# Sending decays and rows from GpSimd, and naming two experts earlier, in a recurrence followed by a routed expert layer

## The chip, the cores and the metric

The kernel runs on one core of a Trainium2 chip. The metric is the device time of one execution in microseconds; the median of three runs of the kernel before is 436.33 us (435.48 to 436.64). The profile is of one more execution.

## The reference

A gated recurrence over 768 steps makes tokens, and each token then goes through one of 16 experts:

```python
q, k, v, f_logit: (4, 8, 768, 48) float32
f = 1 / (1 + exp(-f_logit))
for t in range(768):                       # per batch and head, state is 48 x 48
    state = f[t][:, None] * state + outer(k[t], v[t])
    y[t] = q[t] @ state
x = y.transpose(0, 2, 1, 3).reshape(3072, 384)

g_idx = argmax(x @ w_group)                # 4 groups, softmax weight g_w
e_idx = argmax(x @ w_expert[g_idx])        # 4 experts of the group, softmax weight e_w
out[token] = g_w * e_w * (relu(x @ w1[g, e]) @ w2[g, e])     # w1 384 x 1024, w2 1024 x 384
```

All is float32 in and out. One expert has two weight tensors of 1.5 MB each.

## The kernel before

**The recurrence, in 12 units.** The 768 steps are cut into 6 chunks of 128. A unit is one chunk of two of the four batches: units 2c and 2c+1 make up chunk c. A unit's work is cut into stages, each a generator that emits some instructions at every call: `l` loads f, k, q and v (SyncE's queue, four transfers of 384 KB in rows of 192 bytes), `c` bounds f on VectorE, `g` makes the decays (`gated`: exponential and logarithm on ScalarE, the cumulative sum `cs` as a matmul at L574, two exponentials into `eq` and `kh`, L575 and L576, and a DMA of the last decay row, 4 KB, into `ends`, L581), `m` multiplies q and k by the decays on VectorE (`multiplied`), `t` transposes them on TensorE and copies them out on ScalarE (`turned`, L604 and L605), `s` makes the scores `ap` (L630) and masks them into `am` on VectorE (L633), `n` updates the state, `w` makes the output (`weighed`: matmuls from the state at L669, then from `am` at L674, copied to `xT` at L677), `d` makes the router's logits (`done`: L689, copied to `lgT` at L691, folded at L694), and `x` transposes the output back into token rows (`listed`: L709, copied at L710) and sends 384 KB of them to `x_dram` with a DMA (L712). Stage `b` (`decayed`) transposes the four rows of `ends` of a chunk on TensorE (L614), once in every odd unit.

**The order.** TensorE, VectorE and ScalarE run in the order in which the program emits the stages; the lists `BEGIN`, `EVEN`, `ODD` and `ORDERS` write it down by hand. `"g+1"` is one call of stage g for the next unit. SyncE and GpSimd are ordered by a scheduler from the same program. The queues are strictly in order: a DMA that an engine issues waits in that engine's queue with everything behind it. ScalarE issues the `ends` and `x_dram` transfers, SyncE the loads, the weights and the 4 KB `meta` writes, GpSimd the indirect gathers and scatters.

**Routing.** When both units of a chunk have logits, `routed(c)` starts, a generator that is called by the letter `r`. Its calls are: 1 and 2 the best group and expert as a one-hot `ohe` (L189 to L200); 3 the rank of each token within its expert by matmuls (`rk`, L205 and L208); 4 adds the count so far (L214 to L217); 5 and 6 the operands of a table of token numbers; 7 the routing weight, written with the token's number as `meta` into the last two columns of `x_dram` (L245 to L247: VectorE, a GpSimd copy, a SyncE DMA); 8 the table's matmul (`tb`, L252); then the table is added up.

**The early experts.** After the fourth chunk (`CLOSE` = 3) the two fullest experts are ranked (`ranked`, L272 to L281), named in `who` (L287 to L290), and 128 of their tokens each are taken as `rows_e` (L313 to L319). SyncE reads `who`, and loads each one's `w1` and `w2` (`load_weights`); GpSimd gathers the 128 rows of each from `x_dram` with their `meta` (L394). Calls named `e` then emit: the transposes of the first gather (`turn_in`, L430), of the second, the first layer of both experts (`up`, L440) and the second layer of both (`down_rows`, L457). These stand in the last list, `ORDERS[NU]`, between the routing calls of the last two chunks.

**The experts.** When all is routed, 16 further passes go through the experts, widths 230 down to 174 tokens, each with the two layers (L440 and L472), gathers, transposes in and out on VectorE, and scatters (L451). The weights have two buffers and one more, and are loaded some passes ahead.

Of the kernel before, what the change touches and what calls it, by code (L numbers as in the profile page):

```python
# [23 lines left out]
def kernel(  # L24
# [155 lines left out]
    def route(c, lg, sb, tabled=True, tidy=None, ranking=None):  # L180
# [36 lines left out]
        nc.vector.tensor_tensor(run, run, rk[:, B, :], OP.add)  # L217
        yield
# [94 lines left out]
    def choose_early(sb):  # L313
        number = numbers(sb)
        mine = sb.tile([P, EARLY, GE], FP32, tag="mine2", bufs=1, name="mine2")
        nc.vector.tensor_tensor(mine, order[:, 0:EARLY, :], number[:, :, 0].unsqueeze(1).broadcast_to((P, EARLY, GE)), OP.mult)
        got = sb.tile([P, EARLY], FP32, tag="got2", bufs=1, name="got2")
        nc.vector.reduce_sum(out=got, in_=mine, axis=AX)
        nc.vector.tensor_copy(rows_e, got)  # L319
        named(EARLY, sb)  # L320
# [59 lines left out]

    def load_weights(pool, ap):
        e = value(ap, GE - 1)
        w1 = pool.tile([P, KO, F], FP32, tag="w1", name="w1")
        nc.sync.dma_start(out=w1, in_=w1v[bass.ds(e, 1)].rearrange("o p k f -> (o p) k f"))
        w2 = pool.tile([P, FO, DM], FP32, tag="w2", name="w2")
        nc.sync.dma_start(out=w2, in_=w2v[bass.ds(e, 1)].rearrange("o p k f -> (o p) k f"))
        return w1, w2
# [113 lines left out]
    with ExitStack() as fast:  # L501
# [33 lines left out]

        SRC = {"f": f_logit, "k": k, "qh": q, "v": v}
# [21 lines left out]
        def gated(i):  # L558
# [13 lines left out]
            for b in range(2):  # L572
# [4 lines left out]
                if b:  # L577
# [3 lines left out]
                    nc.scalar.dma_start(out=ends[c][2 * s:2 * s + 2, :], in_=eq[P - 1:P].rearrange("o b h d -> o b (h d)"))  # L581
                yield

        def multiplied(i):

            w = live[i]
            for b in (slice(0, 1), slice(1, 2)) if i < 2 else (slice(0, 2),):
                qh, kh = heads(w["qh"][:, b])[:, :, 0:D], heads(w["kh"][:, b])[:, :, 0:D]
                nc.vector.tensor_tensor(qh, qh, heads(w["eq"][:, b])[:, :, 0:D], OP.mult)
                yield  # L590

                nc.vector.scalar_tensor_tensor(out=kh, in0=kh, scalar=math.exp(SAFE), in1=heads(w["k"][:, b]), op0=OP.min, op1=OP.mult)
                yield

        def turned(i):
# [4 lines left out]
            for b in range(2):  # L600
                for nm in ("q", "k"):
                    pt = bank([P, HP, P], "tr_" + nm)
                    for a in range(HP):
                        nc.tensor.transpose(out=pt[:, a, :], in_=w[nm + "h"][:, b, 2 * a:2 * a + 2, :].rearrange("t r d -> t (r d)"), identity=ident)  # L604
                    (nc.vector.tensor_copy if i == 0 and b == 0 and nm == "k" else nc.scalar.copy)(w["T" + nm][:, b], pt)  # L605
                    yield
# [94 lines left out]
        def listed(i):  # L701
# [10 lines left out]
            nc.scalar.dma_start(out=rows_of(c, 2 * s, 2)[:, :, 0:DM], in_=x.rearrange("t b a r d -> t b (a r d)"))  # L712
            yield

        def routed(c):

            yield from route(c, groups[c], sb, tidy=fix_early if c == CLOSE + 1 else None, ranking=rank_early if c == CLOSE else (lambda pool: ranked(GE, pool)) if c == NC - 1 else None)
            if c == CLOSE:
                choose_early(sb)
                for p in range(EARLY):  # L720
                    weights[p] = load_weights(wp, who[0:1, p:p + 1])
# [5 lines left out]
        def advance(gens):  # L727
# [11 lines left out]
            d0 x1 x1 t2 t2 t2 t2 c3 g3 g3 x1 s2 s2 s2 s2 g3 g3 w2 d1 w2 n2 m3 m3 c4 g4 g4""".split()  # L739
# [4 lines left out]
            NU - 2: "d-2 r r r x-1 x-1 t t t t g+1 g+1 x-1 r s s s s w d-1 w n m+1 m+1 r r".split(),  # L744
            NU - 1: "d-2 b n-1 x-1 x-1 r r t t t t x-1 r s s s s r w d-1 w r r".split(),
# [261 lines left out]
```

## Time and profile before

| | us |
|---|---|
| median of three runs | 436.33 (435.48 to 436.64) |
| the profiled execution's own time | 435.97 |
| its span, first to last instruction | 434.2 |
| TensorE, matmuls busy | 409.4 (94%) |
| TensorE, weight loads busy | 383.8 (88%) |
| VectorE busy | 268.5 (62%) |
| ScalarE busy | 154.5 (36%) |
| GpSimd busy | 71.7 (17%) |
| granted TensorE clock, mean | 0.986 |

The first 145 us are the recurrence and its routing, and the rest is the experts; the early experts lie from 141.9 to about 169.5 us. A line of the timeline holds: start, duration (both us from the span's start), engine, program line, operation, names, shapes, count, and in brackets how long the engine stood idle before it and what released it. PE is TensorE's matmuls, PEld its weight loads, DVE VectorE, ACT ScalarE, POOL GpSimd and SP SyncE; ACTq, POOLq and SPq are these engines' queues, that is instructions that count as no work, such as the issue of a DMA. Matmuls are pipelined and their ends are modelled, so a busy PE says little, while a gap before a PE or PEld line is time in which TensorE had to wait. Line numbers are those of the kernel before.

### The profile page before, as it was taken

The numbers are of one execution on the slowest core, as the hardware profiler recorded it, in microseconds if no ns is written. First come the engines' busy times: TensorE is split into PE (matmuls) and PEld (weight loads), VectorE is DVE, ScalarE is ACT, GpSimd is POOL, SyncE is SP. The second block draws the span as 40 slices with busy tenths as digits, with TensorE's granted clock in tenths as the row PEclk, the third lists the DMA queues.
The fourth block names the chain that finished last, engine by engine and source line by source line (L and its number), as shares of the span: only waits on it lengthen the run. The fifth ranks groups of instructions, "written<-read, shape, count | busy, mean of one in ns | idle before, by whom it ended". The sixth has DMA issues, their size and how long they took to land. (4 is left out here: it accounts for less than half of the span.)

```text
span 434.2 us, 10159 instructions
## 1 busy us (share of the span) xinstructions
PE 409.4 (94%) x4103; PEld 383.8 (88%) x4103; DVE 268.5 (62%) x781; ACT 154.5 (36%) x338; POOL 71.7 (17%) x109
## 2 busy tenths in 40 slices
PE   4999999999998989999999999999999999999960
PEld 2888999889998877989999999999999999999940
DVE  5675786778687841540799759468559558651500
ACT  5676765576664411211123123123123122222200
POOL 3000000000002037101031232212212211022120
PEclk9999999999999999999999999999999999999995
DMA  9999999999815979965728549468459558652010
GB/s 168 175 208 203 186 196 161 219 217 209 159 39 166 404 242 364 394 217 215 255 74 337 170 189 327 151 238 311 158 233 348 174 191 331 239 163 92 25 32 17
DMA packets 135232, 88.97 MB, mean 205 GB/s; under 512 B 105422, under 2 KB 125972, under 8 KB 135178
## 3 DMA queue, kind: packets, MB, share of 16 engines
q1 hardware_dynamic: 126754, 72.38, 61.2%
q0 software_dynamic: 5056, 11.06, 7.6%
q10 hardware_dynamic: 3368, 4.80, 3.1%
q8 instruction: 34, 0.56, 0.6%
q14 instruction: 20, 0.16, 0.1%
HBM read 78.71 MB, written 9.83 MB: 204 GB/s over the span
## 5 line engine op out<-in xcount | busy, mean ns | idle before, releaser
L440 PE MATMUL hp<-xe,w 128*128 128x128 f32 (+14 forms) x864 | 138.6, 320 | 1.6 <-DMA w<-in_moe_w_dram 1.6
L440 PEld LDWEIGHTS hp<-xe,w 128*128 128x128 f32 x864 | 135.8, 190 | 2.5 <-issue 1.7
L472 PE MATMUL yo<-h,w 128*128 128x230 f32 (+13 forms) x672 | 115.8, 333 | 0.0
L472 PEld LDWEIGHTS yo<-h,w 128*128 128x128 f32 x672 | 113.7, 190 | 0.2
L423 DVE STREAM_TRANSPOSE yr<-yT 32x192 f32<-32x192 f32 (+1 forms) x208 | 70.5, 339 | 64.7 <-ACT yT L473 62.1
L441 ACT ACTIVATE h<-hp 128x256 f32<-128x256 f32 (+14 forms) x72 | 34.4, 478 | 110.7 <-PE hp L440 110.7
L416 DVE STREAM_TRANSPOSE xe<-xg 32x192 f32<-32x192 f32 (+1 forms) x208 | 69.7, 335 | 5.0 <-PE hp L440 2.0
L451 POOL DMA_INDIRECT out_dram<-yt,xg x32 | 34.5, 1080 | 154.7 <-ACT yt L448 82.2
L473 ACT COPY yT<-yo 128x230 f32<-128x230 f32 (+13 forms) x42 | 13.5, 326 | 80.5 <-PE yo L472 80.5
L394 POOL DMA_INDIRECT xg<-x_dram,rows_p x30 | 29.6, 988 | 70.4 <-DMA out_dram<-yt,xg 22.8
L633 DVE TENSOR_TENSOR am<-ap,tri 128x512 f32<-128x512 f32 x48 | 29.8, 683 | 18.0 <-PE ap L630 18.0
L574 PE MATMUL cs<-ld_f,tri 128*128 128x384 f32 x48 | 19.2, 526 | 6.2 <-DVE ld_f L555 5.4
L630 PE MATMUL ap<-Tq,Tk 48*64 48x128 f32 x768 | 23.9, 273 | 0.1
L674 PE MATMUL y<-am,v 128*64 128x128 f32 x384 | 23.1, 273 | 0.0
L674 PEld LDWEIGHTS y<-am,v 128*64 128x64 f32 x384 | 21.3, 137 | 0.5 <-DVE am L633 0.5
L630 PEld LDWEIGHTS ap<-Tq,Tk 48*64 48x64 f32 x768 | 20.8, 133 | 1.0 <-issue 0.2
L457 PE MATMUL yo<-w,h 128*128 128x384 f32 x64 | 21.3, 486 | 0.0
L246 POOL COPY meta<-token 128x4 int32<-128x4 int32 x6 | 1.3, 218 | 109.0 <-DMA x_dram<-meta 109.0
L457 PEld LDWEIGHTS yo<-w,h 128*128 128x128 f32 x64 | 11.9, 190 | 7.4
L574 PEld LDWEIGHTS cs<-ld_f,tri 128*128 128x128 f32 x48 | 8.6, 200 | 10.4 <-POOL meta L246 5.4
L448 ACT ACTIVATE yt<-yr,xg 128x384 f32<-128x384 f32 (+13 forms) x26 | 14.4, 604 | 5.4 <-DVE yr L423 5.4
L677 ACT COPY xT<-y 128x512 f32<-128x512 f32 x24 | 12.9, 588 | 8.2 <-PE y L674 8.2
(168 smaller groups left out, 380.4 us busy)
## 6 DMA issues: line engine op xcount, KB each, us to landing
w<-in_moe_w_dram SPq DMA_DIRECT2D x34, 1536.0 KB, 11.0
qh<-in_q_dram SPq DMA_DIRECT2D x12, 384.0 KB, 8.0
ld_k<-in_k_dram SPq DMA_DIRECT2D x12, 384.0 KB, 7.8
v<-in_v_dram SPq DMA_DIRECT2D x12, 384.0 KB, 7.1
x_dram<-x ACTq DMA_DIRECT2D x12, 384.0 KB
ld_f<-in_f_logit_dram SPq DMA_DIRECT2D x11, 384.0 KB, 6.1
out_dram<-yt,xg POOLq DMA_INDIRECT x32, 3.8
xg<-x_dram,rows_p POOLq DMA_INDIRECT x30, 6.6
```

What stands on the lines that cost most here:

```text
L394: nc.gpsimd.indirect_dma_start(out=w["x"][:, j, :], out_offset=None, in_=x_dram[0:1 + top, :], in_offset=bass.IndirectOffsetOnAxis(ap=rows ...
L416: squares(w, lambda n, k_, rk, g, rg: nc.vector.transpose(out=xT[rg, 0:n, k_], in_=x[rk, 0:n, g]))
L423: squares(w, lambda n, k_, rk, g, rg: nc.vector.transpose(out=y[rk, 0:n, g], in_=yT[rg, 0:n, k_]))
L440: nc.tensor.matmul(hp[:, o, :], lhsT=w1[:, ko, (f + o) * P:(f + o + 1) * P], rhs=w["xT"][:, ko, :], start=(ko == 0), stop=(ko == KO - 1))
L441: nc.scalar.activation(h[:, f:f + 2, :], hp, AF.Relu)
L451: nc.gpsimd.indirect_dma_start(out=out, out_offset=bass.IndirectOffsetOnAxis(ap=w["x"][0:m, j, DM + 1:RW].bitcast(U32), axis=0), in_=y[0:m ...
L457: nc.tensor.matmul(yp, lhsT=w["h"][:, fo, :], rhs=w2[:, fo, :], start=(fo == 0), stop=(fo == FO - 1))
L472: nc.tensor.matmul(yp, lhsT=w2[:, fo, m * P:(m + 1) * P], rhs=w["h"][:, fo, :], start=(fo == 0), stop=(fo == FO - 1))
L574: nc.tensor.matmul(cs.rearrange("t h d -> t (h d)"), lhsT=tri, rhs=nl[:, b], start=True, stop=True)
L630: nc.tensor.matmul(ap[r][half, a, :], lhsT=w["Tk"][rows, b, a, half], rhs=w["Tq"][rows, b, a, :], start=True, stop=True)
L633: nc.vector.tensor_tensor(am[:, r], ap[r], tri.unsqueeze(1).broadcast_to((P, HP, P)), OP.mult)
L674: nc.tensor.matmul(ys[r][DP * b:DP * b + DP, a, :], lhsT=w["v"][:, b, 2 * a + r, :], rhs=w["am"][b][:, r, a, :], start=(c == 0 and a == 0) ...
```

## The change

1. `side(i)` is new: in units 0 to 9 the `ends` DMA and the `x_dram` row DMA are issued by GpSimd, not by ScalarE. Units 10 and 11 keep ScalarE.
2. `route` takes `counted`, a function that it calls at the end of call 4. For the fourth chunk it is `load_early`: the ranking, the naming and the weight loads of the two early experts, which came after the table before. `choose_early` no longer names; it makes `rows_e` alone, and the fourth chunk has no ranking call any more, so that the table's matmul, its addition and the choice of rows are one call.
3. The early weights are loaded as w1, w1, w2, w2 (`load_layer`) instead of w1, w2, w1, w2.
4. In unit 0 alone, stages m and t take q of both batches and then k of both, and the copy of the first transposed k moves from VectorE to ScalarE.
5. In `BEGIN` the first half of unit 2's output (`w2`) moves ahead of `g3 g3`.
6. The routing calls in the lists of units 9, 10 and 11 move: in 9 and 10 one stands right behind the four transposes, ahead of the next unit's `cs`; in 11 two stand at the beginning and one right behind the transposes, and the last two calls of unit 10 are gone.

```diff
         nc.vector.tensor_tensor(run, run, rk[:, B, :], OP.add)
+        if counted:
+            counted(sb)
         yield
...
         nc.vector.tensor_copy(rows_e, got)
-        named(EARLY, sb)
...
+    def load_layer(pool, e, layer):
+        w = pool.tile([P, KO, F] if layer == 1 else [P, FO, DM], FP32, tag=f"w{layer}", name=f"w{layer}")
+        nc.sync.dma_start(out=w, in_=(w1v if layer == 1 else w2v)[bass.ds(e, 1)].rearrange("o p k f -> (o p) k f"))
+        return w
...
+        def side(i):
+            return nc.gpsimd if i < NU - 2 else nc.scalar
...
-                    nc.scalar.dma_start(out=ends[c][2 * s:2 * s + 2, :], in_=eq[P - 1:P].rearrange("o b h d -> o b (h d)"))
+                    side(i).dma_start(out=ends[c][2 * s:2 * s + 2, :], in_=eq[P - 1:P].rearrange("o b h d -> o b (h d)"))
...
+        def in_order(i, bs):
+            return [(nm, b) for nm in ("q", "k") for b in bs] if i == 0 else [(nm, b) for b in bs for nm in ("q", "k")]
...
-                    (nc.vector.tensor_copy if i == 0 and b == 0 and nm == "k" else nc.scalar.copy)(w["T" + nm][:, b], pt)
+                nc.scalar.copy(w["T" + nm][:, b], pt)
...
-            nc.scalar.dma_start(out=rows_of(c, 2 * s, 2)[:, :, 0:DM], in_=x.rearrange("t b a r d -> t b (a r d)"))
+            side(i).dma_start(out=rows_of(c, 2 * s, 2)[:, :, 0:DM], in_=x.rearrange("t b a r d -> t b (a r d)"))
...
+        def load_early(pool):
+            rank_early(pool)
+            named(EARLY, pool)
+            es = [value(who[0:1, p:p + 1], GE - 1) for p in range(EARLY)]
+            w1s, w2s = ([load_layer(wp, e, layer) for e in es] for layer in (1, 2))
+            weights.update(enumerate(zip(w1s, w2s)))
...
-                for p in range(EARLY):
-                    weights[p] = load_weights(wp, who[0:1, p:p + 1])
...
-            d0 x1 x1 t2 t2 t2 t2 c3 g3 g3 x1 s2 s2 s2 s2 g3 g3 w2 d1 w2 n2 m3 m3 c4 g4 g4""".split()
+            d0 x1 x1 t2 t2 t2 t2 c3 g3 g3 x1 s2 s2 s2 s2 w2 g3 g3 d1 w2 n2 m3 m3 c4 g4 g4""".split()
...
         ODD = "l+2 d-2 b n-1 r r x-1 x-1 t t t t g+1 g+1 x-1 r s s s s c+2 w d-1 g+2 w g+2 n m+1 m+1 r n".split()
...
-            NU - 2: "d-2 r r r x-1 x-1 t t t t g+1 g+1 x-1 r s s s s w d-1 w n m+1 m+1 r r".split(),
-            NU - 1: "d-2 b n-1 x-1 x-1 r r t t t t x-1 r s s s s r w d-1 w r r".split(),
+            NU - 3: "l+2 d-2 b n-1 r r x-1 x-1 t t t t r g+1 g+1 x-1 r s s s s c+2 w d-1 g+2 w g+2 n m+1 m+1 r n".split(),
+            NU - 2: "d-2 r x-1 x-1 r t t t t r g+1 g+1 x-1 s s s s w d-1 w n m+1 m+1".split(),
+            NU - 1: "d-2 b r r n-1 x-1 x-1 t t t t r x-1 r s s s s w d-1 w r r".split(),
```

The order that comes out of it: on SyncE the two reads of `who` and the four weight loads now stand ahead of the fourth chunk's `meta` write, where they stood behind it; on GpSimd the twenty new DMAs stand between the `meta` copies in the order of the units, and the last of them ahead of the early gathers; on VectorE the ranking and naming stand ahead of unit 9's `am`.

## The prediction

> **What bounds it now.** I read the busy table first.
>
> ```profile
> PE 409.4 (94%) x4103; PEld 383.8 (88%) x4103; DVE 268.5 (62%) x781; ACT 154.5 (36%) x338; POOL 71.7 (17%) x109
> ```
>
> TensorE sets the time, so what counts is where it stands still. Its own timeline gives every gap; leaving out the start (5.38 us) and one of 0.68 at 10.05, there are these:
>
> ```profile
> 13.96 1.56 PE L574 MATMUL cs<-ld_f,tri 128*128 128x384 f32 x4 [0.30 <-ACT ld_f L568]
> 35.73 1.56 PE L574 MATMUL cs<-ld_f,tri 128*128 128x384 f32 x4 [0.51 <-ACT ld_f L568]
> 88.05 1.15 PE L709 MATMUL x_ps<-ident,xT 128*128 128x128 f32 x8 [0.35 <-ACT xT L677]
> 135.84 0.20 PE L205 MATMUL rk<-ohe,strictb 128*128 128x64 bf16 x1 [1.12 <-DVE ohe L200]
> 153.25 5.60 PE L440 MATMUL hp<-xe,w 128*128 128x128 f32 x48 [1.59 <-DMA w<-in_moe_w_dram]
> ```
>
> From 153 to 419.7, where the last matmul ends, there is none: a gain up to there shortens the run one for one. Next the timelines of VectorE and the weight loads in unit 9: scores at 114.78, masks from 115.92 for 2.48 us, and the output's weight loads at 118.38, just as the masks end. A later mask is a later TensorE.
>
> ```profile
> 114.78 1.98 PE L630 MATMUL ap<-Tq,Tk 48*64 48x128 f32 x64
> 115.92 2.48 DVE L633 TENSOR_TENSOR am<-ap,tri 128x512 f32<-128x512 f32 x4 [2.87 <-PE ap L630]
> 118.38 1.78 PEld L674 LDWEIGHTS y<-am,v 128*64 128x64 f32 x32
> ```
>
> Then the queues around the early experts: fourth `meta` issued at 126.17, gather at 133.74 when `rows_e` is there, weights at 134.66, gathered rows used at 141.90; the fifth and sixth `meta` are queued behind weights.
>
> ```profile
> 126.17 0.37 SPq L247 DMA_DIRECT2D x_dram<-meta  x1
> 133.74 1.15 POOL L394 DMA_INDIRECT xg<-x_dram,rows_e  x1 [19.72 <-DVE names L289]
> 134.66 0.40 SPq L384 DMA_DIRECT2D w<-in_moe_w_dram  x1
> 141.90 0.40 PEld L430 LDWEIGHTS xg_ps<-ident,xg 128*128 128x128 f32 x3
> 151.87 0.37 SPq L247 DMA_DIRECT2D x_dram<-meta  x1
> 158.51 0.96 POOL L394 DMA_INDIRECT xg<-x_dram,rows_p  x1 [22.16 <-ACT h L441]
> ```
>
> The table by stretches (last two columns: share of the DMA engines, GB/s) shows the DMA engines empty from 119 to 127 and full with weights from 137 to 155.
>
> ```profile
> 119.00:127.00 8.00, 8.00 (x140) 7.27 (x140) 6.78 (x24) 7.04 (x14) 0.00 (x0) 1.00 0.01 2
> 137.00:155.00 18.00, 16.29 (x241) 15.18 (x234) 15.60 (x65) 5.22 (x14) 0.00 (x0) 1.00 1.04 401
> 155.00:156.00 1.00, 1.00 (x11) 1.00 (x10) 0.96 (x3) 0.25 (x1) 0.00 (x0) 1.00 0.78 111
> ```
>
> Last, ScalarE's queue and the decay rows: an `ends` issue of 0.60 us at 104.03, its reader at 110.11.
>
> ```profile
> 85.59 0.27 ACT L691 COPY lgT<-lT 128x128 f32<-128x128 f32 x1 [3.93 <-DMA ends<-eq]
> 104.03 0.60 ACTq L581 DMA_DIRECT2D ends<-eq  x1
> 110.11 0.41 PE L614 MATMUL gt<-ident,ends 4*128 4x4 f32 x4
> ```
>
> **The change, part by part.** *The twenty DMAs.* ScalarE loses 10 x 0.60 us (L581) and 10 x 0.41 (L712), 10.1 us, and its waits ahead of them (3.93 us at 85.59). TensorE hardly gains, for only the 0.35 us at 88.05 can hang on them, and that gap has a DMA behind it: unit 8's f lands at 86.09 (VectorE waits 1.99 us for it), is bounded in 0.56, goes through the 0.84 us exponential at 86.68, and only then is xT copied, at 87.43. So the gap stays while that load lands where it does: 0. What the moved DMAs can cost: on GpSimd, the `meta` copies are now queued behind row writes, but the third one waits until 72.0 anyhow and SyncE needs it at 107.85: 0. For the decay rows the trace shows no direct DMA of GpSimd; its indirect ones take 3.1 to 8.6 us from issue to landing (gathers; scatters 3.8, median). The scatter is nearest, being a write out of SBUF that isn't behind weights, and 110.11 - 103.9 = 6.2 us are there: 0, at the upper end 2.4 us in each of five odd units.
>
> A rule speaks against this part. The Trainium skill's SBUF page (SBUF: two separate sides) says that GpSimd can't write descriptors while VectorE runs an operation in a 2-port mode. The nearest row is VectorE's bounding of f, 0.56 us once a unit: by it a DMA starts at most 0.56 us later, and by the page's example (some 2.5 us lost) at most 2.5; 3.8 + 2.5 = 6.3 would be 0.1 over the 6.2. No run shows it; I take the row, 0.
>
> *Unit 0 and `w2` ahead of `g3`.* The transposes of q no longer wait behind k's load (landed 9.44); with the copies 0.48 us apart on ScalarE the scores come at about 11.4, not 11.68. Unit 3's gap of 0.51 (0.75 by the weight loads) goes. That is 0.3 to 0.8 us by unit 3, and TensorE then meets unit 8's f at 86.09 sooner and waits there the longer: carried on, 0. The ends: -0.8, if the loads, issued when TensorE frees their buffers, come as much earlier; +1.1, if one more row write goes ahead of that load, since row writes no longer stand in ScalarE's queue (q10 held 10.8% of the engines for 30 us with three of them, 1.1 us each).
>
> *Unit 9.* Rank matmuls stand right behind the transposes; `ohe` ends at 113.05, so they start at 113.10 (+0.08). VectorE starts 0.48 after them (as at 146.98 to 147.46): 113.58. Count 0.81 (L214 to L217 at 120.52 to 121.33), ranking 1.52 (L272 to L281 at 130.92 to 132.44), naming 0.58 (133.36 to 133.94): 116.5. The masks could start at 116.0 and start at 116.5. **+0.6** in all; the 2.87 us for which VectorE stood idle there hide the rest.
>
> *Units 10 and 11.* Unit 10's table operands are ready at 124.4, the transposes end at 124.6, `rows_e` at 126.95, masks wanted at 127.4: 0, with 0.2 to 0.4 to spare. In unit 11 VectorE no longer ranks between 130.92 and 133.9, so `ohe` is there at about 133.9 instead of 135.79, before the transposes end (135.1). The last transpose's weight load ended at 134.49 and `rk` came at 135.84: **-1.35**.
>
> *The early weights.* Names at 116.5; SyncE needed 0.72 from `who` (133.94) to the first issue: 117.2. Data flowed at full rate some 1.9 us after it (137 against 134.66, part of it earlier): 119.1. Four tensors are 6.29 MB, unit 9's row write 0.39: 6.68 / 0.401 = 16.6 us, done at 135.7. The 1.59 us at 153.25 go: **-1.6**.
>
> *What is now behind them.* The fourth `meta` write stands behind four weight loads in SyncE's queue, and the early gathers wait for it. The Trainium skill's page DMA: Bandwidth & Descriptors (Queues, rings and completion order) says that each DMA engine consumes a queue's descriptors in ring order. The rows agree: weights flow until about 155.2, the sixth `meta`, issued at 151.87, is waited for until some 157.6 (by SyncE's next weight load), and the gather starts at 158.51. By the rule the fourth `meta` is complete 2.4 us after the weights, at 138.1, and the gather starts there; if it could pass them it would land at 129 and no gather would be late. The gather lands after 3.1 us at the least (6.0 in the early ones, beside weights; nothing flows now, so I take 3.5): 141.6. TensorE wants it at 141.90 + 0.6 - 1.35 = 141.2: **+0.4** (0 to 2.9). Behind it on TensorE stand unit 11's logits and the last routing; the second gather, 1.25 us later, has 3 us more, and the next experts' weights, which follow that routing, have some 4 us to spare (first tensor due at 174.75, issued at 157.85, 11 to land). The free DMA engines from 136 on cost nothing.
>
> **Sum**, on the profiled execution's 435.97 us: +0.6 - 1.35 - 1.6 + 0.4 = -1.95, so 434.0. The median lies 0.36 above that execution: **434.3 us**.
>
> **Rivals.** *The gathers become the wait* (0.20). `meta` behind weights is late by more: landing in 6.0 us gives 144.1, a stall of 2.9, and 436.8. For it: every gather under load took so long. Against: the engines are empty then. From 1.05 us of stall it is no measurable gain, from 3.65 a loss.
> *The decay rows come late* (0.12), the slower side: at L614 in units 1, 3, 5, 7 and 9 TensorE waits for GpSimd's DMA. It decides from a landing of 6.2 + 3.3 / 5 = 6.9 us; at 7.4 it costs 5 x 1.2 = 6 and gives 440.3. For it: gathers' median of 6.6 under load, and the 2-port rule. Against: 4 KB alone in its queue.
> *The loads come late* (0.13): the +1.1 above, 435.4, within the noise.
> *The first gains carry* (0.15): -0.8, 433.5.
>
> **How the numbers follow.** 0.3% (1.3 us) is about what a measurement of this kernel can tell. The forecast itself has 0.40. Faster: 0.40 + 0.15 = 0.55. Same: 0.13 and 0.12 of the gathers' case: 0.25. Slower: 0.08 and 0.12: 0.20. The forecast's own range is 433.3 to 435.2; to leave out 2 in 10, 432.8 to 438.8 reaches from the carried gains past the late gathers into the late decays.
>
> **What would show it.** No gap before `rk` of unit 11 and none before the second expert's first layer: the steps of unit 11 and of the weights. A wait before unit 9's L674 of about half a us. First weight at about 117, the fourth `meta` done after the last weight, first early gather at about 138 and a gap of up to 1 us before its transposes. The gap at 88 still there. It is wrong if L614 shows gaps, if the gather starts before 130 or lands after 143, or if unit 9 and 10 hold TensorE for more than 1 us.

## The result, and the profile after

The changed kernel takes 437.27 us (median of four runs, 436.71 to 438.26) beside 436.11 for the kernel before (now also four, 435.48 to 436.64): the ratio is 1.003, 95% interval 1.0007 to 1.0053. It is slower, where 434.3 was forecast. The profiled execution took 437.38 us with a span of 435.5; the one before took 435.97 with 434.2. Two more measurements, beside the experiments, gave 1.0059 (1.0037 to 1.0080; e5) and 1.0049 (1.0032 to 1.0066; e6), so the loss is 1.2 to 2.4 us.

TensorE is as busy as before. These lines of its timeline (line numbers are now those of the changed kernel: L574 is L581, L614 L625, L674 L685, L440 L442) hold its gaps of 0.24 us and more after the start, and two places where a gap was:

```profile
42.46 0.38 PE L625 MATMUL gt<-ident,ends 4*128 4x4 f32 x4 [0.64 <-DMA ends<-eq]
51.87 1.31 PE L685 MATMUL y<-am,v 128*64 128x128 f32 x20 [0.24 <-issue]
58.93 0.28 PE L254 MATMUL tb<-val,ln 128*128 128x64 bf16 x4 [0.50 <-DVE val L236]
...
135.66 0.19 PE L205 MATMUL rk<-ohe,strictb 128*128 128x64 bf16 x1
...
139.34 0.66 PE L680 MATMUL y<-Tq,st 48*64 48x128 f32 x15 [0.83 <-issue]
...
143.52 0.52 PE L432 MATMUL xg_ps<-ident,xg 128*128 128x128 f32 x3 [0.40 <-DMA xg<-x_dram,rows_e]
...
152.68 3.48 PE L442 MATMUL hp<-xe,w 128*128 128x128 f32 x29
```

The two large gaps of before are gone as forecast: `rk` of the last unit (1.12 us) and the second early expert's first layer (1.59). New ones stand at `gt` of unit 3, in units 3 and 4, inside `y` of the last unit, and at the early gather. Still, the last matmul ends at 419.13 us, 0.56 sooner than before. Unit 9 and the queues went nearly as worked out:

```profile
115.41 1.98 PE L641 MATMUL ap<-Tq,Tk 48*64 48x128 f32 x64
117.03 2.46 DVE L644 TENSOR_TENSOR am<-ap,tri 128x512 f32<-128x512 f32 x4
119.01 1.93 PEld L685 LDWEIGHTS y<-am,v 128*64 128x64 f32 x31
117.84 7.05 SPq L384 DMA_DIRECT2D w<-in_moe_w_dram  x4
126.42 27.00 SPq L249 DMA_DIRECT2D x_dram<-meta  x3
140.12 1.06 POOL L396 DMA_INDIRECT xg<-x_dram,rows_e  x1 [14.92 <-DVE at L225]
```

The masks stand 1.62 us behind the scores' start (1.14 before), the weights are issued from 117.84 (134.66 before), the fourth `meta` after them at 126.42, and the early gather at 140.12 (138.1 forecast). Of the two stretches in the prediction's table, the one whose DMA engines were empty is now full, and the full one nearly empty:

```profile
119.00:127.00 8.00, 8.00 (x116) 6.96 (x116) 7.46 (x25) 6.73 (x14) 0.93 (x2) 1.00 0.99 371
137.00:155.00 18.00, 16.66 (x240) 15.45 (x231) 13.16 (x52) 5.56 (x14) 2.24 (x3) 1.00 0.25 69
```

What turns 0.56 us of gain into a loss comes behind the last useful instruction. At the end of the program GpSimd goes through an instruction named INC_SWDGE_SEM (the update, below) and a DRAIN, and the other engines wait for it: in the changed kernel it ends at 434.6 us, and their own last DRAINs start from 434.9 on. These are the instructions of the last lines, before and then after (columns: line, queue, operation, count, then min/median/max in ns and the first and last start):

```profile
L953 POOLq INC_SWDGE_SEM  x1: 1464/1464/1464, 426.6 to 426.6; - x1
L1002 POOLq DRAIN  x3: 44/107/5302, 428.1 to 433.9; - x3
```

```profile
L972 POOLq INC_SWDGE_SEM  x1: 1885/1885/1885, 425.8 to 425.8; - x1
L1021 POOLq DRAIN  x3: 46/103/6930, 427.7 to 435.2; - x3
```

The longest of the three DRAINs grew from 5.30 to 6.93 us and the update from 1.46 to 1.89, 2.05 us together, while GpSimd's DMAs went from 64 to 84.

### The profile page after: what moved, and what is told of

Read it like the earlier page. It is cut to its first block, busy times and chain, and to the rows that moved or that the text cites. A ratio compares the mean times of both kernels' runs of the same rounds, so it can differ in the third digit from the quotient of the medians.

```text
span 435.5 us, 10183 instructions
## 1 busy us (share of the span) xinstructions
PE 410.2 (94%) x4103; PEld 384.6 (88%) x4103; DVE 268.3 (62%) x780; ACT 155.0 (36%) x339; POOL 84.5 (19%) x129
## 4 chain that ended last, share of the span: by engine, by line
PE 86%; DMA 6%; DVE 3%; ACT 2%; issue 1%; POOL 0%; POOLq 0%; SPq 0%; DVEq 0%
PE hp L442 31%; PE yo L474 26%; PE yo L459 5%; DMA ld_f<-in_f_logit_dram 4%; PE ap L641 4%; PE y L685 4%; PE cs L581 3%; PE x_ps L720 2%; PE lT L700 2%; PE tr_q L615 2%; PE tr_k L615 2%; PE ds L658 2%; PE y L680 1%; DMA out_dram<-yt,xg 1%; DMA xg<-x_dram,rows_e 1%
## 5 line engine op out<-in xcount | busy, mean ns | idle before, releaser
L442 PE MATMUL hp<-xe,w 128*128 128x128 f32 (+14 forms) x864 | 138.6, 320 | 0.0
L442 PEld LDWEIGHTS hp<-xe,w 128*128 128x128 f32 x864 | 135.8, 190 | 0.8
L581 PE MATMUL cs<-ld_f,tri 128*128 128x384 f32 x48 | 19.4, 529 | 5.7 <-DVE eq L520 5.6
L685 PE MATMUL y<-am,v 128*64 128x128 f32 x384 | 23.6, 273 | 0.2 <-issue 0.2
L685 PEld LDWEIGHTS y<-am,v 128*64 128x64 f32 x384 | 21.5, 137 | 1.2 <-DVE am L644 0.5
L723 POOL DMA_DIRECT2D x_dram<-x x10 | 7.5, 752 | 70.2 <-ACT x L721 55.7
L581 PEld LDWEIGHTS cs<-ld_f,tri 128*128 128x128 f32 x48 | 8.6, 200 | 9.8 <-issue 6.1
```

Source lines behind the costliest of these rows:

```text
L442: nc.tensor.matmul(hp[:, o, :], lhsT=w1[:, ko, (f + o) * P:(f + o + 1) * P], rhs=w["xT"][:, ko, :], start=(ko == 0), stop=(ko == KO - 1))
L581: nc.tensor.matmul(cs.rearrange("t h d -> t (h d)"), lhsT=tri, rhs=nl[:, b], start=True, stop=True)
L685: nc.tensor.matmul(ys[r][DP * b:DP * b + DP, a, :], lhsT=w["v"][:, b, 2 * a + r, :], rhs=w["am"][b][:, r, a, :], start=(c == 0 and a == 0) ...
```

## The experiments

Each ratio is to the kernel before, run on the same chip, with its 95% interval. "Stretch 2 to 4" is the time from the first score matmul (`ap`) of unit 2 to that of unit 4.

### Who sends: e1 to e4

e1 leaves the new order and lets ScalarE send again; e2, e3 and e4 leave the old order and let GpSimd send both, the decays alone, and the rows alone, in units 0 to 9.

```diff
 # e1, on the changed kernel
-            return nc.gpsimd if i < NU - 2 else nc.scalar
+            return nc.scalar
 # e3 on the kernel before; e4 the same at the row DMA, e2 at both
-                    nc.scalar.dma_start(out=ends[c][2 * s:2 * s + 2, :]
+                    (nc.gpsimd if i < NU - 2 else nc.scalar).dma_start(out=ends[c][2 * s:2 * s + 2, :]
```

> The changed kernel with ScalarE sending all decays and rows again; everything else of the change stays. Three theories. CLOSING: GpSimd pays at the end for every DMA that it has sent, in its closing DRAIN (5.30 us before with 64 DMAs, 6.93 after with 84: 0.081 us each) and in the semaphore update ahead of it (1.46 and 1.89 us). With 64 again the DRAIN is 5.2 to 5.4 us and the update 1.4 to 1.5; the execution ends some 1.9 us sooner than the changed kernel, 435.2 to 435.8, at or just under the kernel before. FIRST USE: the moved DMAs cost where their data is awaited (TensorE's 0.64 us at `gt`, 42.5 us), and the longer DRAIN is a chance of one execution: the 0.64 us go, the DRAIN is not tied to the count, 436.6. ORDER: the reordering is what costs, and the sender does not matter: within 0.4 us of the changed kernel, 436.9 to 437.6.

> The kernel before with only the sender changed: decays and rows of units 0 to 9 by GpSimd, no other part of the change. CLOSING: DRAIN 6.8 to 7.0 us and the update 1.8 to 1.95, TensorE's last matmul within 0.7 us of the kernel before, the execution 1.3 to 2.4 us slower: 437.4 to 438.6. FIRST USE: `gt` waits 0.5 us or more in several of its five units, the last matmul 1 us later, DRAIN 5.3: 437.0. ORDER: the kernel before, 435.7 to 436.5.

> The kernel before with the ten decay DMAs alone (4 KB each) sent by GpSimd; the rows stay with ScalarE. It tells what the closing DRAIN counts. If it counts DMAs: 74 of them, 6.1 us, the same as with the ten row DMAs instead. If it counts packets or bytes: the ten decays are a small part of the 1,440 packets and 3.98 MB that the twenty add, 5.3 to 5.5 us. Time by the first 0.9 to 1.1 us over the kernel before, by the second within 0.3 us of it; a wait at `gt` for the decays, if there is any, shows here too.

> The kernel before with the ten row DMAs alone (384 KB each) sent by GpSimd; the decays stay with ScalarE. If the closing DRAIN counts DMAs: 6.1 us, as with the ten decays. If it counts packets or bytes: 6.7 to 6.9 us, nearly the whole of the 1.6. Time by the first 0.9 to 1.1 us over the kernel before, by the second 1.6 us.

| | DMAs of GpSimd | closing DRAIN, us | update, us | time, us | before, us | ratio |
|---|---|---|---|---|---|---|
| e1 | 64 | 5.302 | 1.456 | 443.41 | 437.15 | 1.0142 (1.0122 to 1.0161) |
| e2 | 84 | 6.930 | 1.885 | 440.30 | 437.15 | 1.0080 (1.0059 to 1.0101) |
| e3 | 74 | 6.113 | 1.682 | 439.78 | 437.15 | 1.0054 (1.0035 to 1.0072) |
| e4 | 74 | 6.118 | 1.687 | 439.35 | 437.15 | 1.0047 (1.0030 to 1.0064) |

The closing DRAIN goes with the number of DMAs, not with bytes: ten of 4 KB and ten of 384 KB give the same 6.1 us, and 64, 74 and 84 stand on one line of 0.0814 us each. The closing update adds 0.021. The times of e2 to e4 are 1.1 to 1.6 us more than that bill (2.05, 1.03 and 1.03), and e2 is above the 437.4 to 438.6 that was expected of it: sending from GpSimd costs something earlier too (below).

For e1 all three theories fail: 6.3 us slower, although its DRAIN is as short as foretold. ScalarE's timeline names the place.

```profile
37.66 0.51 ACT L583 ACTIVATE kh<-cs 128x384 f32<-128x384 f32 x1
42.10 0.61 ACTq L588 DMA_DIRECT2D ends<-eq  x1
42.75 0.27 ACT L702 COPY lgT<-lT 128x128 f32<-128x128 f32 x1 [4.58 <-DMA ld_f<-in_f_logit_dram]
```

The decays of unit 3 are ready at 38.2 us and are not sent until 42.1. The semaphore that tells of their completion, number 108, is one of eight that the program names for the DMAs of SyncE and ScalarE and gives out again and again, and its last holder was a load of f, issued at 34.13, that landed at 42.0. ScalarE stands with all that is behind it, and TensorE waits 2.24 us for `lgT` and 2.88 at `gt`. In the kernel before the same DMA gets the semaphore of a load of q, issued at 30.03, and is not held. So the new order loses 6.3 us when ScalarE sends, and GpSimd, whose DMAs have eight other semaphores in this program, avoids the hold. Which part of the order brought the two DMAs together was not tried alone; e18, which undoes the new opening and unit 0, has no such hold.

### The one hold: e8, and the base again: e5

```diff
 # e8, on the changed kernel (e5 is the changed kernel itself)
-            return nc.gpsimd if i < NU - 2 else nc.scalar
+            return nc.gpsimd if i == 3 else nc.scalar
```

> The changed kernel with ScalarE sending again, but for the decays and rows of unit 3, which GpSimd sends. When ScalarE sent them all it stood 4.58 us before the decays of unit 3 (38.2 to 42.7 us): they were given completion semaphore 108, whose last holder was the load of `ld_f` issued at 34.13 us, and that landed at 42.0. SEMAPHORE: that one hold made the order slow; with these two DMAs elsewhere ScalarE is not held for over 1.5 us anywhere, `gt` at 46.4 does not wait 2.88 us, the last matmul comes 4.5 to 6 us sooner than with ScalarE sending all, and with 66 DMAs the closing DRAIN is 5.46 us: 436 to 437.3. QUEUE: if it is ScalarE's load of DMAs in general that the new order can't bear, other units stand as long (over 2 us somewhere) and the time stays over 440.

> The changed kernel as it is, once more, beside the next three on one chip: the base that they are read against, and a second look at the two stalls of its first profile that nothing of the kernel explains, TensorE's break of 0.83 us inside the 32 matmuls of `y` at 139.34 us and `xg_ps` waiting 0.40 us for its gather at 143.5. If the break belongs to the place in the program it is there again within 0.3 us of that time; if it is a chance of one execution it is gone or elsewhere. Time 1.0007 to 1.0053 of the kernel before, as measured first.

e8: 437.29 beside 435.83, ratio 1.0036 (1.0024 to 1.0049), where e1 had 1.0142: the one hold was worth 4.6 us or so. ScalarE no longer stands ahead of `lgT` of unit 3, and the DRAIN is 5.460 us with 66 DMAs. In the profiled execution, a long one (440.10 us), `gt` waited 1.63 us for the decays that GpSimd now sent (issued at 38.0, landed 4.6 us later).

e5: 438.20 beside 435.83, ratio 1.0059. The break inside `y` is back with 0.83 us at 140.53, 3.33 us after the last unit's first scores, as in the first profile (3.32), so it is no chance of one execution. The gather is waited for 1.08 us, and `gt` of unit 3 1.94.

### Settling the account earlier: e6, e7, e9, e10

If the closing DRAIN works off an account, another DRAIN while GpSimd is idle should take most of it.

```diff
 # e9 on the kernel before, e10 on the changed kernel, in the loop over the passes
+        if n == GE - 3:
+            with tc.issue_after(sent[-1].ins):      # sent: the scatters so far
+                nc.gpsimd.drain(fusable=False)
         past, coming = ws.pop(n - 1, None), ws.get(n + 2)
```

> The changed kernel with one DRAIN of GpSimd put in its queue at the head of the pass before the last two experts (about 384 us), where GpSimd is idle for over 9 us. CLOSING: a DRAIN settles the account of all DMAs sent until then, so the one in the middle takes 77 x 0.0814 = 6.3 us beside TensorE's matmuls and the closing one only some 7 x 0.0814 + 0.09 = 0.7 us instead of 6.93, the update ahead of it 0.15 to 0.5 instead of 1.89; TensorE's last matmul stays where it is; the execution is 7 to 8 us shorter than the changed kernel: 429.5 to 430.5 if the kernel before takes 436.1 to 437.2. If the closing DRAIN's length is something else that goes with the number of DMAs (a table that is cleared whatever was cleared before), it stays at 6.9 and the time is that of the changed kernel.

> The kernel before with the same single DRAIN at the same place. CLOSING: in the middle 57 x 0.0814 = 4.7 us, closing DRAIN 0.7 us instead of 5.30, the update 0.15 to 0.5 instead of 1.46; 5.6 to 6 us shorter than the kernel before: 430.3 to 431.3. With it the bill of the twenty moved DMAs is hidden in both kernels, so the changed kernel with the DRAIN beats this one by what its order gained until the last matmul: 0.56 us by the two first profiles (half a microsecond either way). Without any effect of the DRAIN: the kernel before.

> The kernel before with one DRAIN of GpSimd in its queue, this time tied behind the scatter ahead of it so that it stays there: seven DMAs come after it. CLOSING as an account that any DRAIN settles: near 385 to 400 us a DRAIN of about 57 x 0.0814 = 4.6 us beside TensorE's matmuls, the closing one 7 x 0.0814 + 0.09 = 0.66 us instead of 5.30 and the update 0.3 instead of 1.46: 5.3 to 5.9 us shorter than the kernel before. CLOSING as a fixed bill per DMA of the whole program, whatever ran before: 5.30 again, the time of the kernel before.

> The changed kernel with the same DRAIN, tied in the same way. As an account that any DRAIN settles: in the middle about 77 x 0.0814 = 6.3 us, at the end 0.66 instead of 6.93, the update 0.3 instead of 1.89; 7.2 to 7.9 us shorter than the changed kernel and, since both kernels then end alike, within 1 us of the kernel before with the DRAIN: what is left between the two is the order and the waits until the last matmul (by the profiles so far between 0.6 us sooner and 1.9 us later). As a fixed bill: the time of the changed kernel.

e6 and e7 were written without `issue_after` and `fusable`, and nothing held the DRAIN in its place: it ran at 3.5 us, for 0.76 and 0.70 us, before GpSimd had sent any DMA. There it settles nothing. The closing DRAIN is 6.93 and 5.30 us as without it, and so is the time: 437.85 beside 435.83 for the changed kernel (the 1.0049 above), and 435.93, ratio 0.9999 (0.9987 to 1.0012), for the kernel before. Their profiles are read below as second ones of either kernel. In e9 and e10 the DRAIN is in its place. First the two DRAIN lines of e9 (L853 in the middle, L1007 at the end), then those of e10:

```profile
L853 POOLq DRAIN  x1: 10496/10496/10496, 383.6 to 383.6; - x1
L1007 POOLq DRAIN  x3: 46/107/1680, 426.9 to 429.4; - x3
```

```profile
L872 POOLq DRAIN  x1: 11372/11372/11372, 383.4 to 383.4; - x1
L1026 POOLq DRAIN  x3: 46/103/1604, 426.2 to 428.8; - x3
```

The one in the middle takes 10.5 and 11.4 us instead of the 4.6 and 6.3 worked out, beside matmuls that go on; a scatter was under way when it began. The closing one falls to 1.7 and 1.6 us (0.66 was worked out) and the update to 0.33 and 0.35. So a DRAIN in the middle takes most of the bill away, but with one there the 0.0814 us for each DMA gives neither of the two lengths, and why is open. e9 takes 431.72 beside 436.20, ratio 0.9902 (0.9879 to 0.9926), e10 431.55, ratio 0.9904 (0.9884 to 0.9924). Both beat both kernels, and the change is now worth nothing: with the bill of the twenty DMAs hidden, new and old kernel are the same within the noise.

### Units 3 and 4: e11, e13, e17

In the profiles in which GpSimd sends, stretch 2 to 4 takes 25.4 to 27.5 us, and 24.6 in three profiles of the kernel before. e11 sends the decays of unit 3 sooner, e13 queues the rows later (with the DRAIN of e10), e17 gives the decays back to ScalarE (with the DRAIN and the `meta` of e12).

```diff
 # e11
-... s2 s2 s2 s2 w2 g3 g3 d1 w2 n2 ...
+... s2 s2 s2 s2 g3 g3 w2 d1 w2 n2 ...
 # e13
-            side(i).dma_start(out=rows_of(c, 2 * s, 2)[:, :, 0:DM], in_=...)
+            with tc.issue_after(out_ends[max(out_ends)].ins) if max(out_ends) < NU - 2 else nullcontext():
+                side(i).dma_start(out=rows_of(c, 2 * s, 2)[:, :, 0:DM], in_=...)
 # e17
-                    side(i).dma_start(out=ends[c][2 * s:2 * s + 2, :], in_=...)
+                    nc.scalar.dma_start(out=ends[c][2 * s:2 * s + 2, :], in_=...)
```

> The changed kernel with the opening's order of unit 3 put back: its decays (the second `g3`) are computed and sent ahead of `w2`, some 0.5 us sooner. DECAYS: `gt` of unit 3 waited 0.64, 1.94 and 0.97 us for the decays that GpSimd sends, because GpSimd's DMA lands 3.0 to 5.6 us after its issue and `w2` stands ahead of it; half a microsecond sooner takes half a microsecond of the wait, so `gt` waits 0 to 1.4, and the execution is 0.3 to 0.6 us shorter. LOADS: what is late in units 3 and 4 is the load behind it, and the wait at `gt` only takes the place of one at the next unit; then the stretch from the scores of unit 2 to those of unit 4 stays at 25.7 to 27.5 us (24.6 before) and the time at that of the changed kernel.

> The changed kernel with the settling DRAIN, and each row DMA of GpSimd queued behind the decay DMA that stands ahead of it in the written order, as ScalarE's queue held it in the kernel before. ROWS: where GpSimd sends, the rows of unit 2 leave at 44.9 to 45.9 us instead of 48.2 to 48.9, the loads' queue moves 8 to 56 KB in the microsecond of their peak instead of some 150, and the `ld_f` of unit 5 is clamped at 51.7 to 53.2 instead of 50.2 to 50.8. With the rows leaving at 48 or later it is clamped before 51.2, the stretch from the scores of unit 2 to those of unit 4 is 24.6 to 25.2 us instead of 25.7 to 27.5, and the execution is 0.7 to 1.3 us shorter than the changed kernel with the DRAIN alone: 430.2 to 430.9 if the kernel before takes 436.2. OTHER: if what is late comes from another thing, the stretch stays at 25.7 or more and the time is 431.5.

> The changed kernel with the settling DRAIN and the early `meta` by GpSimd, and the decays sent by ScalarE again; the rows stay with GpSimd. Here the completion semaphore of unit 3's decays was last held by the decays of unit 2, not by a load. DECAYS: `gt` of unit 3 does not wait for them (under 0.2 us), TensorE's clock stays at full speed from 12 to 420 us, the stretch from the scores of unit 2 to those of unit 4 is 24.6 to 26.2 us (with rows alone by GpSimd it was 26.15 in the kernel before) instead of 26.8, and the time 0.5 to 1.8 us under that with the decays by GpSimd: 429.6 to 430.9 where the kernel before takes 435.9. OTHER: the wait at `gt` stays or another of over 1 us comes in the same unit: 431.4 or more.

e11: `gt` waits 0.36 us, the stretch is 25.84, the time 438.17 beside 436.20, ratio 1.0050 (1.0030 to 1.0070): no gain. e13: the rows of unit 2 leave at 49.7 instead of 45, the f of unit 5 is clamped at 52.0, the stretch is 26.9 with 1.33 us at `gt`, and the time is 432.80 beside 435.93, ratio 0.9924 (0.9900 to 0.9949). VectorE came to the clamp only then and did not wait for the load, so this profile does not decide on rows that push the load aside. The one of e14 (below) does: its rows also leave late, at 49.2, and VectorE still waits 1.19 us for f, until 51.99. That theory falls. e17: `gt` waits 0.28 us and the clock stays up, but 0.60 us appear ahead of `rk` of the same unit, the stretch is 26.17, and the time is 433.33 beside 437.44, ratio 0.9925 (0.9901 to 0.9949). So rows alone, decays alone and both cost here 0.8 us or more, and none of the three edits gave it back.

Where it goes shows when the starts of TensorE's instructions are set beside those of the kernel before. With the decays alone (e3) the whole loss is the wait at `gt`, 0.85 us. With the rows alone (e4) it is a break of 1.11 us inside `y` of unit 3, and 0.38 at `tb`, whose operand `val` VectorE makes after a wait of 1.97 us for the f of unit 5 (0.21 in the kernel before). In the changed kernel, in the mean of four profiles (the first, e5, e6, e10), `gt` costs 1.10, `tb` 0.49, a lower clock 0.38 (last section), the break 0.32 and the rest 0.12; `w2` ahead of `g3` gains 0.74 of that back. An edit that takes one of them leaves or lengthens another: in e11 `gt` costs 0.43 and the break 0.83. Why the f of unit 5 comes late is not settled; it is clamped at 51.6 to 53.2 us wherever GpSimd sends, at 50.2 to 50.8 in the kernel before.

### The early table: e12, e14, e16

```diff
 # e12; e16 with the DRAIN of e10; e14 with the DRAIN and the rows of e13
-        nc.sync.dma_start(out=rows_of(c)[:, :, DM:RW], in_=meta)
+        (nc.gpsimd if c == CLOSE else nc.sync).dma_start(out=rows_of(c)[:, :, DM:RW], in_=meta)
```

> The changed kernel with the fourth chunk's `meta` (L249) sent by GpSimd instead of SyncE, where it stands behind four weight loads. QUEUE: the early gathers wait for that write to land (139.2 in the profile of the change, 13 us after its issue at 126.4); by GpSimd it lands some 4 to 5 us after its issue, so the first gather starts at 131 to 133 instead of 140.1, `xg_ps` does not wait for it (0.40, 1.08, 0.56 us before), and the execution is 0.4 to 1 us shorter, 0.1 of it given back to the closing DRAIN. NAMES: if it is the row numbers, or the rows of the last units, that the gathers wait for, they start at 139 or later as before and nothing is won. In both TensorE's break inside `y` at 139 to 140 stays.

> The same with the fourth chunk's `meta` sent by GpSimd too, which won about 1 us in the profile of its own run (the stretch from the last unit's scores to the first `xg_ps` 6.39 us instead of 7.1 to 8.2). If both gains add up: 429.3 to 430.2, 6.0 to 6.9 under the kernel before. If GpSimd's queue, in which `meta` now stands behind row DMAs that wait for decays, gives it back: the first gather later than 133 us and no gain over the rows alone.

> The changed kernel with the settling DRAIN and `meta` of the fourth chunk by GpSimd, the rows as the change sends them. If the earlier table is worth what its profile showed, 0.6 to 1 us less than with the DRAIN alone, 430.5 to 431; if the gain was a chance of that profile, 431.5. Against the run with the rows later it tells what each is worth.

In e16's timeline of GpSimd the write goes out at 127.69 and the gather starts 5.6 us sooner than in the changed kernel (in e12 at 133.63):

```profile
127.69 0.76 POOL L249 DMA_DIRECT2D x_dram<-meta  x1 [1.68 <-issue]
134.52 1.06 POOL L396 DMA_INDIRECT xg<-x_dram,rows_e  x1 [6.07 <-DVE lgs L708]
```

`xg_ps` waits for nothing in any of the three, and the time from the last unit's scores to it falls from 7.1 to 8.2 us to 6.4 to 6.7: the `meta` behind the weights was the wait. e12 takes 437.57 beside 436.20, ratio 1.0039 (1.0018 to 1.0061), e16 431.39 beside 435.93, ratio 0.9882 (0.9863 to 0.9901), the fastest of all; e14 432.28, ratio 0.9913 (0.9891 to 0.9936). Each by itself is within the noise of the kernel without it.

### The break inside `y`: e15

```diff
+            if i == 0:                                   # ahead of the first cs
+                pt = bank([P, 4], "idle")
+                for _ in range(48):
+                    nc.tensor.matmul(pt[0:16], lhsT=ident[:, 0:16], rhs=ident[:, 0:4], start=True, stop=True)
```

> The changed kernel with 48 matmuls of no use (16 x 4, never read) in TensorE's queue ahead of the first `cs`, where it is idle until 5.4 us. They cost nothing there, but every later instruction of TensorE stands 96 places further on in its program. PLACE: the break sits at a position of the program (17 of the 32 matmuls of `y` done in five of seven profiles, the 15 others after it), so it moves some 48 matmuls ahead, into the scores of the last unit or the work before them, or vanishes; inside `y` at 139 there is none over 0.15 us. DATA: if what `y` reads comes late, the break stays inside `y` at 138.5 to 140.5 us.

```profile
138.27 1.05 PE L684 MATMUL y<-Tq,st 48*64 48x128 f32 x32
...
143.94 0.52 PE L432 MATMUL xg_ps<-ident,xg 128*128 128x128 f32 x3 [1.50 <-DMA xg<-x_dram,rows_e]
```

All 32 matmuls of `y` run in one piece: the break is not a wait for what `y` reads, and in this one profile it vanished with the shift, as it would if it belonged to a position in TensorE's program. It bought nothing, since TensorE then waits 1.50 us for the gather (437.79 us, one run).

What TensorE lacks at that position was not tested. The page counts 34 transfers on an instruction queue (q8), 0.56 MB in all, and the Trainium skill's page Runtime: NRT & Kernel Launch (Instruction fetch mechanics) says that an engine fetches its program in blocks of 16 KiB and that this is mostly hidden. The traces point the same way. Up to 150 us they have 23 breaks of 0.24 us and more inside a stage's matmuls for which the profile names no releaser (`issue`), in 14 profiles, that of `y` in unit 3 among them. All 23 end 1.24 to 1.58 us after one of these transfers has landed; in the first profile of the change it lands at 137.97 and `y` goes on at 139.34. But no run moved the transfers alone, and in e15 one lands at 137.91 without a break behind it.

### The order without GpSimd: e18

Old opening and unit 0, ScalarE sends, early naming and the last units as in the change, with the DRAIN and the `meta` of e16.

```diff
 # on the changed kernel, with the edits of e1, e11 and e16, and in unit 0 (there VectorE also copies the first k again)
-            return [(nm, b) for nm in ("q", "k") for b in bs] if i == 0 else [(nm, b) for b in bs for nm in ("q", "k")]
+            return [(nm, b) for b in bs for nm in ("q", "k")]
```

> The early naming, the order of the loads and of the last three units, the early `meta` by GpSimd and the settling DRAIN, with decays and rows by ScalarE and the opening and unit 0 as in the kernel before. ADDS: up to unit 8 it runs as the kernel before does (24.6 us from the scores of unit 2 to those of unit 4), then gains what the profiles of the new order gained: 2.0 at the early weights, 0.7 to 1.2 in the last unit, less 0.5 in units 9 and 10 and 0.3 to 0.8 for the break inside `y`: 1.5 to 2.5 under the kernel before with the DRAIN (431.7 beside 436.2), 429 to 430.3. LOST: if the gain needs what GpSimd took from ScalarE, the last units or the loads are held by ScalarE's queue instead and it is 431 or more.

433.53 beside 437.44, ratio 0.9911 (0.9886 to 0.9936), no better than the kernel before with the DRAIN (0.9902). Stretch 2 to 4 is 24.70 us. The early weights gain their 1.7 us, but 0.51 us of break and 0.85 at the last `gt` take part of it, and on this chip TensorE stood 1.57 us at 175 to 177 us, in the first layer of the first pass, while the weights flowed; the profile names no cause. That is the chip: from the start of that layer to the last matmul all six profiles taken on it (e1 to e4, e17, e18) need 252.1 to 252.9 us, the other fourteen 250.35. The kernel before, not profiled there, also takes some 1.2 us longer on it (437.15 and 437.44 beside 435.8 to 436.2), so it probably has the like, and times from different chips should not be compared.

## Why the prediction was wrong, point by point

The stretches of three profiles of the kernel before (the first, e7, e9) and four of the changed one (the first, e5, e6, e10; the last row without e9 and e10) beside the steps of the forecast, in us:

| from, to | before | changed | difference | forecast |
|---|---|---|---|---|
| start, scores of unit 0 | 11.53 | 11.78 | +0.25 | 0 |
| to scores of unit 2 | 21.53 | 21.15 | -0.38 | 0 |
| to scores of unit 4 | 24.61 | 26.28 | +1.67 | 0 |
| to scores of unit 8 | 45.30 | 45.10 | -0.20 | 0 |
| to scores of unit 11 | 32.91 | 32.39 | -0.52 | +0.6 - 1.35 |
| to the first `xg_ps` | 5.80 | 7.63 | +1.83 | +0.4 |
| to the first layer of the first pass | 27.30 | 25.25 | -2.05 | -1.6 |
| to the end of the last matmul | 250.35 | 250.35 | 0 | 0 |
| to the end of the span | 14.44 | 16.34 | +1.90 | 0 |
| sum | | | +2.50 | -1.95 |

The forecast's own figures, 435.97 - 1.95 + 0.36, make 434.4, not 434.3; nothing hangs on it.

- **The twenty DMAs at 0** is the step that failed, twice. The forecast costed their issue, ScalarE's relief and their landing, and stopped at the last matmul. The bill at the end of the program, 2.05 us in DRAIN and update, is shown: it follows the count over 64, 66, 74, 84 and 85 DMAs, and a DRAIN in mid-program takes most of it away. The second cost lies in units 3 and 4, 1.67 us, and is taken apart above. The DRAIN of 5.30 us was in the trace of before, outside the chain of waits and the busy table.
- **"6.2 us are there" for the decays** was read in unit 9 and taken for all odd units. In unit 3 the kernel before has less:

```profile
37.96 0.60 ACTq L581 DMA_DIRECT2D ends<-eq  x1
...
42.28 0.41 PE L614 MATMUL gt<-ident,ends 4*128 4x4 f32 x4
```

  That is 4.3 us, and the change itself puts `w2` ahead. GpSimd's 4 KB DMA lands 3.0, 4.2 and 5.2 us (minimum, median, maximum) after its issue in the first profile, so the median of scatters, 3.8, was a fair estimate and the room was wrong. TensorE waited there 0.56 to 1.94 us: the rival of late decays, at one unit and not at five. Its 1.10 us are the largest part of the loss there, but not the whole.
- **The rule on GpSimd's descriptors**, from the SBUF page, bounded the landing at 6.3 us; the decays landed within 5.2, 5.6 and 6.3 in the first three profiles of the change, and no run here separates a part for VectorE's 2-port modes.
- **`w2` ahead of `g3` and unit 0 at 0**: the 0.3 to 0.8 us by unit 3 are there: the last matmul ahead of its `gt` comes 0.74 us sooner after unit 2's scores, and the gap of 0.51 at 35.73 is gone. They were not carried on, as forecast, but it was the wait for the decays at 42 us that took them, not the load of unit 8's f. That unit 0's scores come sooner does not show: +0.25 in the mean.
- **Unit 9, +0.6**: 0.10 and 0.38 us by the next two scores. Right.
- **Units 10 and 11, -1.35**: the stretch between the scores of units 10 and 11 falls by 1.0 (10.57 to 9.56). Right, smaller.
- **The early weights, -1.6**: right. The gap is in no profile of the new order. It gives 1.73 of the 2.05 us; the other 0.32 belong to the gather, next.
- **The gathers, +0.4**: the idle time at `xg_ps` was 0.40, 0.56, 0.58 and 1.08 us, and e12 shows its cause to be the one named, the `meta` behind the weights in SyncE's queue, as the rule of ring order said. But the stretch lost 1.83. The starts of its instructions, before and then after, give the whole:

```profile
138.01 1.05 PE L669 MATMUL y<-Tq,st 48*64 48x128 f32 x32
138.99 1.09 PE L689 MATMUL lT<-xT,gw 128*64 128x128 f32 x16
...
141.76 0.41 PE L694 MATMUL lg<-fold,lgT 128*128 128x40 f32 x2
142.01 0.52 PE L430 MATMUL xg_ps<-ident,xg 128*128 128x128 f32 x3
```

```profile
137.81 0.70 PE L680 MATMUL y<-Tq,st 48*64 48x128 f32 x17
...
139.94 1.09 PE L700 MATMUL lT<-xT,gw 128*64 128x128 f32 x16
...
142.71 0.41 PE L705 MATMUL lg<-fold,lgT 128*128 128x40 f32 x2
143.52 0.52 PE L432 MATMUL xg_ps<-ident,xg 128*128 128x128 f32 x3 [0.40 <-DMA xg<-x_dram,rows_e]
```

  From `y` to `lT` it is 2.13 us instead of 0.98, from `lg` to `xg_ps` 0.81 instead of 0.25; in the mean of the four profiles the break costs 1.01 and the late gather 0.83, more than the idle times printed, which count from modelled ends. After a late gather the matmuls of `lT` behind it take 0.32 less (1.02 us from their start to that of `x_ps`; about 1.34 before, and in e12, e14 and e16, where nothing waits). So the gather costs 0.5 net, about the price of the forecast, and the break inside `y` is what was not foreseen.
- **The gap at 88 us** was said to stay; it is in none of the first three profiles of the change, and not in e7 and e9, which are the kernel before up to there; in e3 and e14 it is 1.54 and 1.77 us. So it was not a fixed part of the kernel.

The rivals were each half right: the gathers did become a wait, at the price of the forecast and not of the rival, and the decays came late in one unit. Neither alone gives the result, and the loss at the end was in none of them.

The gains, some 3 us in the table, came nearly as worked out and were spent in three places: in units 3 and 4, in the last unit, and at the end of the program. The forecast had the first as a rival at the wrong units, of the second the gather alone, and of the third nothing.

## What to carry to other kernels

Moving DMAs to GpSimd has a price that neither the busy table nor the chain of waits of this profile showed: in this kernel its closing DRAIN and semaphore update grew by 0.10 us per DMA sent, behind the last result. Read the instructions after the last useful one before costing such a move at nothing; if GpSimd has an idle stretch, a DRAIN of its own there, tied to its place, took 4.5 us from the kernel before and 6 to 7 from the changed one. And read the slack of a moved transfer in every unit, for the first units are not like the later ones.

## What the runs showed of the hardware that was not expected

- A short wait can cost twice. When `gt` of unit 3 waited 1.21 to 1.94 us (e5, e13, e15, e16), TensorE's granted clock was 0.5 for one stretch of 3.4 us after it, and the next sixteen transposes took nearly double. The same followed 1.54 us of waiting at 89 us in e3 and 1.69 at 80 us in e8. The timeline of e13 and its table by stretches (last three columns: granted clock, share of the DMA engines, GB/s):

```profile
42.16 0.38 PE L627 MATMUL gt<-ident,ends 4*128 4x4 f32 x4 [1.33 <-DMA ends<-eq]
42.47 1.23 PE L722 MATMUL x_ps<-ident,xT 128*128 128x128 f32 x8
43.49 1.06 PE L617 MATMUL tr_q<-ident,qh 128*128 128x128 f32 x4
```

```profile
40.00:43.00 3.00, 1.67 (x29) 1.51 (x26) 1.13 (x3) 1.13 (x2) 0.00 (x0) 1.00 0.98 194
43.00:47.00 4.00, 4.00 (x23) 4.00 (x21) 1.89 (x7) 3.51 (x8) 0.00 (x0) 0.57 1.43 165
```

  Four transposes take 1.06 us here and 0.60 in the first profile of the change; from the first of them to `cs` it is 3.33 us instead of 1.75. The Trainium skill's page TensorE: Matmul & The Clock Gate (Part 1: The HAM clock gate) says that the clock falls to half after at least one idle window of about 3.4 us. The length of the slow stretch agrees; the idle time doesn't, for 1.2 us were enough here, while other waits of 1.26 to 1.77 us (before at 153 us, e14 at 90, e8 at this very `gt`) left the clock at full speed. So the wait's length alone does not decide it, and what does is open. In all six the slow stretch begins a whole number of its own lengths of 3.41 us after the clock first rose: ten in e5, e13, e15 and e16, 24 in e3, 21 in e8.
- DMAs of SyncE and ScalarE share eight completion semaphores in this program (numbers 100 to 106 and 108), and a DMA whose semaphore is still held by a slow load stands, with its engine's whole queue behind it: 4.0 us in e1, from a reorder on other engines.
